# Loading each 128-token chunk of q, k and v head by head, one contiguous 32 KB block per transfer

## The chip, the cores and the metric

The kernel runs on one core of one Trainium2 chip. The metric is the device time of one execution in microseconds (us). A run has a profile as well; its **span** is the time from the first to the last instruction of the program and is 1.6 to 2.2 us shorter than the run's time in all runs below. Fast executions of one kernel differ by up to 2%, and each job ran the kernel before again on its own chip (133.4 to 136.5 us), so changed kernels are compared with the runs of before of the same job.

## The reference, cut to what matters

The first half is a retention recurrence over q, k, v of shape (4 batches, 8 heads, 768 tokens, 64), the second a token mixer on its output.

```python
for t in range(S):
    state = gamma[None, :, None, None] * state + np.einsum('bhd,bhe->bhde', k[:, :, t], v[:, :, t])
    y[:, :, t] = scale * np.einsum('bhd,bhde->bhe', q[:, :, t], state)
# ... y is rearranged to x[b, s, h*d]
W_tok = scale * np.einsum('bsd,btd->bst', x @ w_q, x @ w_k)   # 1 / sqrt(64), as above
return (np.maximum(np.einsum('bst,btd->bsd', W_tok, x), 0.0) @ w_out)
```

## The kernel before

The recurrence is worked in chunks of 128 tokens: 4 batches x 6 chunks = 24 chunks. A chunk of q, k or v becomes a tile of 128 partitions (tokens) by 8 heads x 64 floats. In HBM the head is the outer dimension, so within one head the 128 tokens of a chunk are contiguous (128 x 64 x 4 bytes = 32 KB), and the eight heads are eight such blocks. One load takes all eight:

```python
    def emit_dma(i):                       # chunk i
        b, c = divmod(i, NCH)
        q_st = stage_pool.tile([128, H, D], FP32, name="q_st", tag="stage")   # 15 buffers: 5 chunks
        # ... k_st, v_st likewise
        nc.sync.dma_start(
            out=q_st,
            in_=q[b, :, c * C : (c + 1) * C, :].rearrange("h t d -> t h d"),
        )
        # ... k and v likewise, 256 KB each
```

GpSimd scales and casts q and k to bf16 and ScalarE casts v; TensorE transposes, scores and accumulates; VectorE and ScalarE empty its results. The stores of the mixer go through the same queue (SyncE's, called SP in the profile) as the loads:

```python
            nc.sync.dma_start(out=out[b, tc_i * C : (tc_i + 1) * C, :], in_=o_st)   # [128, 512] f32, 256 KB
    # ...
    for i in range(NG):
        # ... emit_dma(i + 3), emit_cast(i + 2), emit_tr(i + 1), emit_scores(i), emit_y(i - 1), ...
        # ... and, in iterations 1 to 4 of a batch, the mixer and the stores of the batch before
```

The queue carries its instructions out in order: in the trace before, a store stands from 54.83 us, the two after it wait for their results and start at 58.31 and 58.76, and the next load starts behind them, at 59.23. Eight completion semaphores are used in turn (in the trace before, 99 DMAs on 101 to 106, 108 and 110), so that a DMA waits until the DMA eight before it has landed: each of the 91 from the ninth on waits for the semaphore of the DMA eight before it, and none was issued before that had landed.

Of the kernel before, what the change touches and what calls it, by code (L numbers as in the profile page):

```python
# [17 lines left out]
def kernel(  # L18
# [10 lines left out]
    nc = tc.nc  # L29

    B, H, S, D = q.shape
    DM = moe_w_out.shape[0]
    DH = moe_w_q.shape[1]
    C = 128
# [37 lines left out]
    for c in range(NCH):  # L72
        nc.vector.tensor_scalar_mul(
            out=txln[:, c, :], in0=ln_gamma, scalar1=tvals_f[:, c : c + 1]
# [9 lines left out]
        out=cmask,  # L84
        in_=cmask,
# [9 lines left out]
    for i in range(NUM_U):  # L95
# [15 lines left out]
        out=wout_stage, in_=moe_w_out.rearrange("(a p) m -> p a m", p=128)  # L111
# [16 lines left out]
    def emit_dma(i):  # L128
        b, c = divmod(i, NCH)
        st = cctx[i]  # L130
        q_st = stage_pool.tile([128, H, D], FP32, name="q_st", tag="stage")
        k_st = stage_pool.tile([128, H, D], FP32, name="k_st", tag="stage")
        v_st = stage_pool.tile([128, H, D], FP32, name="v_st", tag="stage")
        nc.sync.dma_start(  # L134
            out=q_st,
            in_=q[b, :, c * C : (c + 1) * C, :].rearrange("h t d -> t h d"),
        )
        nc.sync.dma_start(  # L138
            out=k_st,
            in_=k[b, :, c * C : (c + 1) * C, :].rearrange("h t d -> t h d"),  # L140
        )
        nc.sync.dma_start(  # L142
            out=v_st,
            in_=v[b, :, c * C : (c + 1) * C, :].rearrange("h t d -> t h d"),
        )
        st["q_st"] = q_st
        st["k_st"] = k_st
        st["v_st"] = v_st
# [250 lines left out]

    alloc_batch(0)  # L400
    emit_dma(0)
    emit_dma(1)
    emit_cast(0)
    emit_dma(2)
    emit_cast(1)
    emit_tr(0)

    for i in range(NG):
        b, c = divmod(i, NCH)
# [60 lines left out]
```

## Time and profile before

| | before |
|---|---|
| time, median of 2 runs | 136.5 us (135.25 to 137.76) |
| span of the profiled run | 132.4 us |
| TensorE (PE) busy | 97.8 us, 74% of the span |
| load instructions on SyncE's queue | 72, of 256 KB |
| median from issue to landing | 4.2 to 4.3 us |
| packets on the load queue | 79,920 |
| share of the 16 DMA engines' time | 79.6% |

From the list of what SyncE's queue itself waited for (us in total, times, longest): the stores stand between the loads and wait for their results.

```profile
SPq L391 <- DVE o_st L388: 32.1, 8, 11.3
```

Of these 32 us the most lie after the last load, where nothing is behind them; the others delay loads.

### The profile page before, as it was taken

The page shows a single profiled execution, that of the slowest core. Times are in us where ns is not written, and L with a number is a line of the kernel's source. Part 1 is how long each engine was busy: PE and PEld are TensorE (multiplying, and loading weights), DVE is VectorE, ACT ScalarE, POOL GpSimd, SP SyncE. Part 2 cuts the span into 40 slices and gives each one's busy share as a digit, 9 for nine tenths or more (in the row PEclk, how much of TensorE's full clock was granted, in tenths as well). Part 3 has the DMA queues.
Part 4 walks back from the last instruction along what each step waited for, and adds up shares of the span by engine and source line. Part 5 has one row for each costly group of instructions (what it writes and reads, how often), then busy time and mean ns, then how long its engine had stood idle before and what let it go on. Part 6 is the DMA issues. An engine that isn't in the chain of part 4 may idle for free.

```text
span 132.4 us, 2906 instructions
## 1 busy us (share of the span) xinstructions
PE 97.8 (74%) x1128; PEld 64.1 (48%) x1128; DVE 78.6 (59%) x141; ACT 58.3 (44%) x127; POOL 50.9 (38%) x65
## 2 busy tenths in 40 slices
PE   0003679765699899981799899861999999977970
PEld 0002558544478466560476556541675556653320
DVE  4061654975767599393457797590637797551830
ACT  3002454653556645382315757362325657413430
POOL 4009755467627654240765550425754200000000
PEclk9999999999999999999779999998569999999999
DMA  3899999999979998959999839959998006600074
GB/s 83 289 272 247 240 245 228 225 246 246 270 168 229 240 226 261 237 168 272 254 244 251 196 83 303 251 172 268 260 223 197 0 4 235 241 0 0 5 296 179
DMA packets 79933, 26.66 MB, mean 201 GB/s; under 512 B 76336, under 2 KB 76336, under 8 KB 79920
## 3 DMA queue, kind: packets, MB, share of 16 engines
q1 hardware_dynamic: 79920, 26.48, 79.6%
q8 instruction: 9, 0.15, 0.4%
q14 instruction: 4, 0.03, 0.1%
HBM read 20.19 MB, written 6.29 MB: 200 GB/s over the span
## 4 chain that ended last, share of the span: by engine, by line
PE 52%; SPq 16%; DMA 13%; ACT 4%; DVE 4%; POOL 4%; issue 3%; POOLq 0%; ACTq 0%; DVEq 0%
PE o_ps L379 13%; DMA q_st<-in_q_dram 12%; SPq L142 6%; PE wqt_ps L308 6%; PE z_ps L342 5%; PE mx_ps L358 4%; PE at_ps L211 4%; SPq L134 4%; PE tr_ps L181 3%; PE xt_ps L285 3%; PE y_ps L269 3%; SPq L138 3%; POOL qs L156 3%; PE wk_ps L322 3%; PE y_ps L261 3%
## 5 line engine op out<-in xcount | busy, mean ns | idle before, releaser
L221 DVE TENSOR_TENSOR at_sb<-at_ps,cmask 128x512 bf16<-128x512 f32 x48 | 31.0, 684 | 25.0 <-PE at_ps L211 25.0
L156 POOL TENSOR_TENSOR qs<-q_st,fq 128x512 bf16<-128x512 f32 x24 | 25.0, 1042 | 48.2 <-DMA q_st<-in_q_dram 33.3
L276 ACT CAST x_nat<-y_ps 128x512 bf16<-128x512 f32 x24 | 14.0, 585 | 29.5 <-PE y_ps L269 29.4
L162 POOL TENSOR_TENSOR ks<-k_st,fk 128x512 bf16<-128x512 f32 x24 | 25.0, 1042 | 3.6 <-DMA k_st<-in_k_dram 2.5
L181 PE MATMUL tr_ps<-identity,qs 128*128 128x128 bf16 x96 | 10.5, 239 | 20.4 <-POOL qs L156 20.3
L379 PE MATMUL o_ps<-wout_sb,relu_mx 128*128 128x512 bf16 x96 | 22.4, 379 | 0.0
L199 DVE COPY qkt<-tr_ps 128x1024 bf16<-128x1024 bf16 x24 | 16.4, 681 | 4.3 <-PE tr_ps L190 4.3
L181 PEld LDWEIGHTS <-qs 128*128 128x128 bf16 x96 | 6.9, 106 | 23.7 <-POOL qs L156 21.6
L168 ACT ACTIVATE vs<-v_st 128x512 bf16<-128x512 f32 x24 | 15.2, 632 | 0.3 <-DMA v_st<-in_v_dram 0.3
L367 DVE TENSOR_SCALAR relu_mx<-mx_ps 128x512 bf16<-128x512 f32 x16 | 9.9, 683 | 8.0 <-PE mx_ps L358 8.0
L379 PEld LDWEIGHTS <-relu_mx 128*128 128x128 bf16 x96 | 8.9, 98 | 9.8 <-DVE relu_mx L367 1.1
L238 PE MATMUL state_ps<-vs,ks 128*128 128x128 bf16 x80 | 8.6, 232 | 4.8 <-ACT vs L168 2.8
L190 PE MATMUL tr_ps<-identity,ks 128*128 128x128 bf16 x96 | 10.7, 242 | 1.1 <-POOL ks L162 1.1
L269 PE MATMUL y_ps<-vs,at_sb 128*128 128x64 bf16 x192 | 11.1, 201 | 0.0
L247 ACT CAST u_tile<-state_ps 64x256 bf16<-64x256 f32 x20 | 7.3, 365 | 8.3 <-PE state_ps L238 8.3
L211 PE MATMUL at_ps<-qkt 64*128 64x128 bf16 x192 | 10.6, 233 | 0.4 <-DVE qkt L199 0.4
L285 PE MATMUL xt_ps<-identity,x_nat 128*128 128x128 bf16 x96 | 10.0, 228 | 1.2 <-ACT x_nat L276 1.1
L388 DVE COPY o_st<-o_ps 128x512 f32<-128x512 f32 x12 | 8.2, 686 | 3.8 <-PE o_ps L379 2.1
L390 ACT COPY o_st<-o_ps 128x512 f32<-128x512 f32 x12 | 7.0, 584 | 7.3 <-PE o_ps L379 5.7
L308 PE MATMUL wqt_ps<-x_t,wq_sb 128*64 128x256 bf16 x48 | 9.2, 342 | 0.3 <-DVE x_t L296 0.3
L238 PEld LDWEIGHTS <-ks 128*128 128x128 bf16 x80 | 5.9, 105 | 7.1 <-issue 7.0
L261 PE MATMUL y_ps<-u_tile,qkt 128*128 128x128 bf16 x80 | 9.3, 226 | 0.0
(37 smaller groups left out, 101.1 us busy)
## 6 DMA issues: line engine op xcount, KB each, us to landing
q_st<-in_q_dram SPq DMA_DIRECT2D x24, 256.0 KB, 4.3
k_st<-in_k_dram SPq DMA_DIRECT2D x24, 256.0 KB, 4.2
v_st<-in_v_dram SPq DMA_DIRECT2D x24, 256.0 KB, 4.3
out_dram<-o_st SPq DMA_DIRECT2D x24, 256.0 KB, 2.3
wout_stage<-in_moe_w_out_dram SPq DMA_DIRECT2D x1, 1024.0 KB, 5.9
wq_stage<-in_moe_w_q_dram SPq DMA_DIRECT2D x1, 128.0 KB, 2.2
wk_stage<-in_moe_w_k_dram SPq DMA_DIRECT2D x1, 128.0 KB, 2.4
```

Source lines behind the costliest of these rows:

```text
L156: nc.gpsimd.tensor_tensor(out=qs, in0=st["q_st"], in1=fq[:, c, :].to_broadcast([128, H, D]), op=ALU.mult,)
L162: nc.gpsimd.tensor_tensor(out=ks, in0=st["k_st"], in1=fk[:, c, :].to_broadcast([128, H, D]), op=ALU.mult,)
L168: nc.scalar.activation(out=vs, in_=st["v_st"], func=ACT.Copy, scale=float(attn_scale))
L181: nc.tensor.matmul(out=tr_ps[:, hp, :], lhsT=qs[:, 2 * hp : 2 * hp + 2, :], rhs=identity, is_transpose=True, start=True, stop=True,)
L199: nc.vector.tensor_copy(out=qkt, in_=tr_ps)
L211: nc.tensor.matmul(out=ps[:, j, :], lhsT=kT(qkt, h), rhs=qT(qkt, h), start=(j == 0), stop=(j == 3),)
L221: nc.vector.tensor_tensor(out=at_sb_par[:, parity, :, :], in0=at_ps[parity], in1=cmask.to_broadcast([128, 4, C]), op=ALU.mult,)
L238: nc.tensor.matmul(out=state_ps[:, hp, :, :], lhsT=ks[:, 2 * hp : 2 * hp + 2, :], rhs=vs[:, 2 * hp : 2 * hp + 2, :], start=(c == 0 and hp ...
L269: nc.tensor.matmul(out=y_ps[:, h, :], lhsT=at_sb[:, h, :], rhs=vs[:, h, :], start=(c == 0 and h == 0), stop=(h == H - 1),)
L276: nc.scalar.copy(out=x_nats[b][:, c, :], in_=y_ps)
L308: nc.tensor.matmul(out=wqt_ps, lhsT=wq_sb[:, dmc, :], rhs=x_t[:, dmc, blk * 2 * C : (blk + 1) * 2 * C], start=(dmc == 0), stop=(dmc == NDM ...
L379: nc.tensor.matmul(out=o_ps, lhsT=relu_mx[:, dmc, tc_i * C : (tc_i + 1) * C], rhs=wout_sb[:, dmc, :], start=(dmc == 0), stop=(dmc == NDM - 1),
```

## The change

The intent: each transfer reads one unbroken 32 KB block of HBM in place of eight blocks. Nothing else changes.

```diff
-        nc.sync.dma_start(
-            out=q_st,
-            in_=q[b, :, c * C : (c + 1) * C, :].rearrange("h t d -> t h d"),
-        )
+        for h in range(H):
+            nc.sync.dma_start(
+                out=q_st[:, h, :], in_=q[b, h, c * C : (c + 1) * C, :]
+            )
 # ... the same for k and v
```

More of the change, by code (lines that the diff above doesn't have):

```diff
@@ L133, in emit_dma @@
         v_st = stage_pool.tile([128, H, D], FP32, name="v_st", tag="stage")
-        nc.sync.dma_start(
-            out=q_st,
-            in_=q[b, :, c * C : (c + 1) * C, :].rearrange("h t d -> t h d"),
-        )
-        nc.sync.dma_start(
-            out=k_st,
-            in_=k[b, :, c * C : (c + 1) * C, :].rearrange("h t d -> t h d"),
-        )
-        nc.sync.dma_start(
-            out=v_st,
-            in_=v[b, :, c * C : (c + 1) * C, :].rearrange("h t d -> t h d"),
-        )
+        for h in range(H):
+            nc.sync.dma_start(
+                out=q_st[:, h, :], in_=q[b, h, c * C : (c + 1) * C, :]
+            )
+        for h in range(H):
+            nc.sync.dma_start(
+                out=k_st[:, h, :], in_=k[b, h, c * C : (c + 1) * C, :]
+            )
+        for h in range(H):
+            nc.sync.dma_start(
+                out=v_st[:, h, :], in_=v[b, h, c * C : (c + 1) * C, :]
+            )
         st["q_st"] = q_st
```

## The prediction

> **What bounds the kernel now.** I read the page from the engines to the transfers, then the chain of work that ended last, then the issues and the SyncE queue's own timeline. First the page: busy time by engine, the slices in time, the packets, the chain.
>
> ```profile
> PE 97.8 (74%) x1128; PEld 64.1 (48%) x1128; DVE 78.6 (59%) x141; ACT 58.3 (44%) x127; POOL 50.9 (38%) x65
> ...
> DMA  3899999999979998959999839959998006600074
> GB/s 83 289 272 247 240 245 228 225 246 246 270 168 229 240 226 261 237 168 272 254 244 251 196 83 303 251 172 268 260 223 197 0 4 235 241 0 0 5 296 179
> DMA packets 79933, 26.66 MB, mean 201 GB/s; under 512 B 76336, under 2 KB 76336, under 8 KB 79920
> ...
> q1 hardware_dynamic: 79920, 26.48, 79.6%
> ...
> PE 52%; SPq 16%; DMA 13%; ACT 4%; DVE 4%; POOL 4%; issue 3%; POOLq 0%; ACTq 0%; DVEq 0%
> ```
>
> No engine is full (PE 74%). The DMA row reads 8 or 9 for most of the first 31 of 40 slices (3.31 us each, so to about 103 us), at roughly 250 GB/s: while loads run, the transfers set the pace, and the last 29 us are PE work on what was loaded. The packet count can be taken apart exactly. 72 loads x 8 heads x 128 tokens is 73,728 packets of 256 B; the two small weights make 1,024 more; 99 DMAs with 16 completion packets each make 1,584. The sum is 76,336, the "under 512 B" figure to the unit. So today's load is already cut into 256 B pieces, one token of one head. In the chain, SPq and DMA together have 29% of 132.4 us, 38 us: no better way of loading can save more along this chain.
>
> The list of issues, with KB each and median us to landing:
>
> ```profile
> q_st<-in_q_dram SPq DMA_DIRECT2D x24, 256.0 KB, 4.3
> k_st<-in_k_dram SPq DMA_DIRECT2D x24, 256.0 KB, 4.2
> v_st<-in_v_dram SPq DMA_DIRECT2D x24, 256.0 KB, 4.3
> out_dram<-o_st SPq DMA_DIRECT2D x24, 256.0 KB, 2.3
> wout_stage<-in_moe_w_out_dram SPq DMA_DIRECT2D x1, 1024.0 KB, 5.9
> wq_stage<-in_moe_w_q_dram SPq DMA_DIRECT2D x1, 128.0 KB, 2.2
> ```
>
> And what one issue holds the SyncE queue for (timeline of that queue; start, us held, what, count):
>
> ```profile
> 22.63 1.62 SPq L142 DMA_DIRECT2D v_st<-in_v_dram  x1
> 24.34 0.86 SPq L134 DMA_DIRECT2D q_st<-in_q_dram  x1
> ...
> 50.67 0.38 SPq L391 DMA_DIRECT2D out_dram<-o_st  x1
> ...
> 58.31 0.36 SPq L391 DMA_DIRECT2D out_dram<-o_st  x1
> 59.23 0.41 SPq L134 DMA_DIRECT2D q_st<-in_q_dram  x1
> ...
> 125.71 0.33 SPq L391 DMA_DIRECT2D out_dram<-o_st  x1
> ```
>
> These rows carry the prediction. With transfers backed up (22 to 25 us) a 1,024-piece load holds the queue 0.8 to 1.6 us[...]. Directly after a pause (59.23) the same 1,024-piece load takes 0.41 us, and a 128-row store 0.33 to 0.38. An eighth of the pieces saves under 0.1 us: an issue costs about 0.35 us **per instruction**, nearly whatever it moves.
>
> [...]
>
> **The change part by part.**
>
> Removed: 72 load issues of 256 KB. Added: 72 x 8 = 576 issues of 32 KB. All stay on the SyncE queue; the instruction listing shows 601 rows on it instead of 101.
>
> Pieces: the HBM side becomes contiguous, but the tile still takes 64 floats, 256 B, into each of 128 partitions, so I expect the same 73,728 packets of 256 B, plus (603 - 99) x 16 = 8,064 completion packets: 87,984 on the load queue. One load gives each DMA engine 8 + 1 packets. Between 20 and 50 us the queue moved 232 GB/s with the engines full, 256 B x 16 / 232 GB/s = 17.7 ns per packet; 9 of them are 0.16 us. The transfer is then shorter than its issue, and the DMA engines sit idle over half of the time.
>
> Pitch of issues: a load behind another starts 0.04 to 0.05 us after it ends (first rows of that timeline: 2.38 + 0.51 to 2.93, 7.70 + 0.85 to 8.60). The closest likeness to the new load is the 128-row store: 0.38 back to back, 0.36 or 0.33 after a pause. I choose 0.38 + 0.05 = **0.43 us**. Two stores in a row stood 0.45 us apart (50.22, 50.67), with one wait more each.
>
> Load stream: 576 x 0.43 = 247.7 us. Ahead of the last load lie 12 stores of the first two batches, 12 x 0.45 = 5.4 us. First load issued at 2.4 us. Last load issued at about 255.5, landed 2 us later (2.2 us for today's 128 KB weight on a free queue): 257.5 us. I add nothing for stores that block the queue (32 us today waiting for o_st): a chunk now comes every 24 x 0.43 = 10.3 us, while PE's work for one is 97.8 / 24 = 4.1 us, and in the listing what those stores need hangs on a chunk loaded at least 10 us earlier.
>
> Tail: only the last chunk's remaining work follows. Before, its scores began at 113.2 and the span ended at 132.4: 19.2 us of scores, transposes, the last batch's mixer, stores. v lands last and goes through one 0.63 us cast. PE has been half idle, and after idle waits its transposes took 0.40 us per four instead of 0.22 (63.78 against 69.22 in the chain), so I add 1 us for a slow start. 257.5 + 0.6 + 19.2 + 1 = 278.3 us of span.
>
> Before, the timed median exceeds the span by 136.5 - 132.4 = 4.1 us. Sum: **282 us**, about 2.07 times the time before. None of the added issue time is hidden: the queue needs 248 us for loads alone, more than the whole kernel today. What it gives back, the load wait of 38 us in the chain, is already gone from this sum, because PE's earlier work lies inside the load stream.
>
> **The rivals.**
>
> A. The contiguous reads pay: pieces merge into larger ones and the DMA-bound first 100 us shrink. For it: 250 GB/s is well under the 303 GB/s of one slice. Against: SBUF's side stays at 256 B, and the issue cost stands anyway. Taken alone, without issue cost, it would give at best 136.5 - 38 = 98 us.
>
> B. Issue time is per piece, not per instruction. For it: the usual 0.85 us for 1,024 pieces, 0.11 us for 128; then 576 x 0.11 = 63 us hide beside transfers and the time stays within 2%, 134 to 139 us. Against: 0.41 us for 1,024 pieces on a free queue and 0.33 for 128 rows.
>
> C. Latency takes over from issue. In the listing each DMA waits until the DMA eight before it has landed, so at most 8 x 32 KB are in flight where it was 8 x 256 KB. If a landing still took 4.3 us, the pitch would be 4.3 / 8 = 0.54 us, and 576 of them 310 us: about 344 us in all. Against: landing on a free queue is 2.0 to 2.4 us, a pitch of 0.25 to 0.30, below the issue's own.
>
> D. The pitch is nearer the first issues of the program (0.43 to 0.58 us): at 0.52 us it is 300 us of loads and about 334 in all. For the low end, 0.33 + 0.04 = 0.37 us, loads take 213 us and the whole 247.
>
> **Range and chances.** Everything but the pitch sums to about 34 us. The pitch from 0.38 to 0.50 us gives 253 to 322; I set 252 to 322 for 8 in 10, the middle at 282. Faster by 2% would need both the issue rows and the packet count misread: 0.01. Within 2% needs rival B: 0.02. Slower: 0.97.
>
> **What would show it right or wrong.** Right: 576 load issues of 0.33 to 0.42 us standing back to back from 2.4 to about 255 us; DMA row at 3 to 5 throughout, about 75 GB/s; landing near 2 us; about 87,984 packets on the load queue; the chain mostly SPq at the load lines, with PE only in the last 20 us; PE busy under 45%. Rival C shows as landings over 3.4 us and the queue waiting on DMA; rival A as fewer packets or over 300 GB/s in a window; rival B as issues of about 0.1 us. The point fails if the small load's issue differs from the store's, or if stores block the queue for many us.

The 282 us are 2.4 + 247.7 + 5.4 to the last issue (255.5), 2 for its landing, 0.6 + 19.2 + 1 of tail and 4.1 from span to time, and the pitch of 0.43 us is the 0.38 + 0.05 read from the trace. The completion packets are the packets of 4 B on the load queue: 1,584 before and 9,648 after, 16 per DMA, and after there are as many semaphore updates by DMAs (9,648). The 8 + 1 packets per DMA engine are an estimate, the 144 packets of a load divided by the 16 engines of the page; the trace does not tell a packet's engine.

## The result, and the profile after

The changed kernel takes **317.32 us** (316.88 and 317.77), against 136.5 us: slower by a factor of 2.33 (2.28 to 2.39). Ratios here are the mean time of one kernel's fast runs over that of the other's of the same rounds, so they are not quite the ratio of the medians quoted. Executions over 1.5% slower than the fastest of the same kernel are left out of the means. Kernels are compared only within the same rounds.

The page of the profile after: engines, slices in time, packets, load queue, and the shares of the chain that ended last.

```profile
PE 135.2 (43%) x1128; PEld 83.4 (26%) x1128; DVE 82.4 (26%) x141; ACT 61.5 (20%) x127; POOL 51.5 (16%) x65
...
DMA  6333332333322332333244332333253522332515
GB/s 196 67 70 69 69 70 62 69 69 69 69 64 60 70 68 62 70 69 69 60 153 132 92 71 62 69 68 71 63 155 68 154 65 65 70 69 63 182 51 202
DMA packets 88003, 26.74 MB, mean 85 GB/s; under 512 B 84400, under 2 KB 84400, under 8 KB 87984
...
q1 hardware_dynamic: 87984, 26.52, 33.7%
...
SPq 79%; issue 9%; DMA 4%; PE 4%; DVE 1%; ACT 1%; POOLq 0%; POOL 0%; ACTq 0%
```

Where the DMA row read 8 or 9 it now reads 2 or 3: the DMA engines have nothing to do for two thirds of the time, and no compute engine is over 43% busy. The chain is the SyncE queue, 79% of the span, which was 16%. PE's busy time rose by 37 us with the same 1,128 matmuls, because each takes longer (300 ns in the mean, 248 before); the row of the granted clock reads 5 to 7 tenths over much of the second half (0.62 to 0.67 in the stretches from 150 to 290 us). PE is not in the way, with 4% of the chain, so this costs little.

The list of issues of the profile after (count, KB each, median us to landing), and one line's own view (duration of one in ns, least, median, longest):

```profile
q_st<-in_q_dram SPq DMA_DIRECT2D x192, 32.0 KB, 1.9
```

```profile
L135 SPq DMA_DIRECT2D q_st<-in_q_dram x192: 327/430/1587, 2.4 to 285.1; - x192
```

And the chain in order of time, at the start of the last q and k loads (start, us, what):

```profile
281.33 0.43 SPq L143
281.76 0.05 issue
281.81 0.02 SPq L135
281.83 0.03 issue
281.86 0.38 SPq L135
282.23 0.04 issue
282.28 0.43 SPq L135
282.71 0.04 issue
282.75 0.43 SPq L135
...
288.92 3.17 DMA k_st<-in_k_dram
```

This is the whole loss in small: 0.43 us of issue and 0.04 us before the next, 0.47 us from start to start, and nothing else between. It goes on from 2.4 us to the last load at 294.1 us. A landing takes 1.9 us from issue, while the load that waits for it comes eight places, 8 x 0.474 = 3.8 us, later: the limit of eight in flight does not bind.

The trace holds every packet. The median 256 B packet took 18 ns before and 18 ns after (means 18.0 and 17.4 ns; 74,752 packets in each). **The contiguous blocks made no packet faster.** The load before reads the same eight 32 KB blocks, and both cut them into 256 B, one head's floats of one token. In these two traces a data packet of the load queue is as long as the run that is unbroken both in HBM and within one partition of the tile: 256 B for the loads, and 2 KB for the 24 stores and the weight w_out (3,584 packets), although each store writes one unbroken 256 KB block of HBM.

Where the 182.5 us between the two spans come from: before, 98.4 us until the last load is issued and 34.0 after it; after, 294.1 us and 20.9. The load stream grew by 196 us, and the tail gave back 13, since less work is still waiting when the last chunk arrives.

### The profile page after: what moved, and what is told of

It is laid out like the page before. It is cut to its first block, busy times and chain, and to the rows that moved or that the text cites. A ratio compares the mean times of both kernels' runs of the same rounds, so it can differ in the third digit from the quotient of the medians.

```text
span 314.9 us, 3693 instructions
## 1 busy us (share of the span) xinstructions
PE 135.2 (43%) x1128; PEld 83.4 (26%) x1128; DVE 82.4 (26%) x141; ACT 61.5 (20%) x127; POOL 51.5 (16%) x65
## 2 busy tenths in 40 slices
DMA packets 88003, 26.74 MB, mean 85 GB/s; under 512 B 84400, under 2 KB 84400, under 8 KB 87984
## 3 DMA queue, kind: packets, MB, share of 16 engines
q1 hardware_dynamic: 87984, 26.52, 33.7%
## 4 chain that ended last, share of the span: by engine, by line
SPq 79%; issue 9%; DMA 4%; PE 4%; DVE 1%; ACT 1%; POOLq 0%; POOL 0%; ACTq 0%
SPq L135 26%; SPq L139 26%; SPq L143 25%; DMA wout_stage<-in_moe_w_out_dram 2%; SPq L391 2%; PE o_ps L379 1%; DMA k_st<-in_k_dram 1%; DMA out_dram<-o_st 1%; DMA v_st<-in_v_dram 0%; PE z_ps L342 0%; PE mx_ps L358 0%; DVE at_sb L221 0%; POOLq L465 0%; PE wqt_ps L308 0%; POOL ks L162 0%
## 5 line engine op out<-in xcount | busy, mean ns | idle before, releaser
L181 PE MATMUL tr_ps<-identity,qs 128*128 128x128 bf16 x96 | 14.2, 300 | 119.8 <-POOL qs L156 119.8
L379 PE MATMUL o_ps<-wout_sb,relu_mx 128*128 128x512 bf16 x96 | 29.5, 451 | 0.0
L238 PE MATMUL state_ps<-vs,ks 128*128 128x128 bf16 x80 | 11.1, 274 | 31.4 <-ACT vs L168 31.4
L190 PE MATMUL tr_ps<-identity,ks 128*128 128x128 bf16 x96 | 13.5, 289 | 19.8 <-POOL ks L162 19.5
L238 PEld LDWEIGHTS <-ks 128*128 128x128 bf16 x80 | 8.1, 124 | 35.1 <-issue 34.8
L190 PEld LDWEIGHTS <-ks 128*128 128x128 bf16 x96 | 8.3, 127 | 27.7 <-POOL ks L162 26.9
L269 PE MATMUL y_ps<-vs,at_sb 128*128 128x64 bf16 x192 | 14.8, 240 | 0.4 <-DVE at_sb L221 0.4
L211 PE MATMUL at_ps<-qkt 64*128 64x128 bf16 x192 | 14.6, 301 | 0.0
L285 PE MATMUL xt_ps<-identity,x_nat 128*128 128x128 bf16 x96 | 14.2, 301 | 0.5 <-ACT x_nat L276 0.5
L269 PEld LDWEIGHTS <-at_sb 128*128 128x128 bf16 x192 | 12.9, 133 | 1.4 <-issue 0.8
L388 DVE COPY o_st<-o_ps 128x512 f32<-128x512 f32 x12 | 8.2, 691 | 13.4 <-PE o_ps L379 7.6
L296 DVE COPY x_t<-xt_ps 128x1024 bf16<-128x1024 bf16 x12 | 8.3, 692 | 12.9 <-PE xt_ps L285 12.9
```

What stands on the lines that cost most here:

```text
L181: nc.tensor.matmul(out=tr_ps[:, hp, :], lhsT=qs[:, 2 * hp : 2 * hp + 2, :], rhs=identity, is_transpose=True, start=True, stop=True,)
L190: nc.tensor.matmul(out=tr_ps[:, HP + hp, :], lhsT=ks[:, 2 * hp : 2 * hp + 2, :], rhs=identity, is_transpose=True, start=True, stop=True,)
L238: nc.tensor.matmul(out=state_ps[:, hp, :, :], lhsT=ks[:, 2 * hp : 2 * hp + 2, :], rhs=vs[:, 2 * hp : 2 * hp + 2, :], start=(c == 0 and hp ...
L269: nc.tensor.matmul(out=y_ps[:, h, :], lhsT=at_sb[:, h, :], rhs=vs[:, h, :], start=(c == 0 and h == 0), stop=(h == H - 1),)
L379: nc.tensor.matmul(out=o_ps, lhsT=relu_mx[:, dmc, tc_i * C : (tc_i + 1) * C], rhs=wout_sb[:, dmc, :], start=(dmc == 0), stop=(dmc == NDM - 1),
```

## The experiments

The theory: an issue costs its queue some 0.47 us whatever it moves, and 576 of them in one queue are the time. The rivals: the cost goes with the pieces; contiguous or small reads are themselves slow or fast; the limit of eight in flight; something that all queues share. Twelve kernels were run; all gave correct results.

### Fewer, larger issues: two heads per load

```diff
-        for h in range(H):
-            nc.sync.dma_start(out=q_st[:, h, :], in_=q[b, h, c * C : (c + 1) * C, :])
+        for h in range(0, H, 2):
+            nc.sync.dma_start(out=q_st[:, h : h + 2, :],
+                in_=q[b, h : h + 2, c * C : (c + 1) * C, :].rearrange("h t d -> t h d"))
```

> Two heads per load: 288 loads of 64 KB (256 pieces of 256 B each) in place of 576 of 32 KB. Theory 'cost per issue on the SyncE queue' (0.474 us start to start, nearly whatever a load moves): 288 x 0.474 = 136.5 us of loads, + 12 stores 5.6, + about 6 us of scattered stalls, + 2.4 start, + 2 landing, + 19 tail: span about 172 us, time 170 to 182, issues still about 0.43 us long. Rival 'cost per 256 B piece in the issue': the number of pieces is unchanged, so the issues double in length to about 0.86 us and the time stays near 317. Rival 'eight loads in flight': no change of pitch at all as long as a landing (1.9 us) is under eight pitches; if it were the limit, pitch stays and time halves likewise, so this run does not test that one.

Measured: 191.8 us (191.3 and 192.3), 1.44 times before (1.427 to 1.457). The issue line's view:

```profile
L135 SPq DMA_DIRECT2D q_st<-in_q_dram x96: 396/468/1591, 2.4 to 162.9; - x96
```

Twice the pieces lengthen an issue from 430 to 468 ns, not to 860: the cost is per instruction, and the rival of cost per piece falls. The time lies 10 us above the expected range and the span, 190.5 us, 18.5 above the expected 172. Of these, 11 are the pitch (start to start), which was 0.512 us and not 0.474: 288 x 0.038 = 11 us; the others are about 5.5 us of stalls beyond the 6 allowed for, and a tail 2 us longer. So an issue isn't quite independent of what it moves.

### Four heads per load

The same edit with steps of 4.

> Four heads per load: 144 loads of 128 KB. Theory: 144 x 0.474 = 68 us of issue, below the about 83 us that the DMA engines need for the 73,728 pieces (18 ns each over 16 engines), so the transfers bound it again and the time is that of the kernel before within 2 to 3%: 134 to 141 us. Rival 'splitting as such costs' (completion packets, waits, smaller loads): between the two, above 145 us. Rival 'contiguity pays, when issue does not hide it' : it would show as under 133 us, though this load is only half way there (32 KB blocks, four per load).

Measured: fast runs 135.5 and 137.5 us, ratio 1.026 (1.012 to 1.041); median of all four runs 137.9 us, two of them slow. The pitch is 0.55 us; 144 x 0.55 = 79 us of issue, about what the DMA engines need (an estimate of 83 us, 73,728 packets of 18 ns over 16 engines), so the queue and the transfers are level, and the profile (a slow run) reads 217 and 221 GB/s in the stretches from 20 to 50 and from 60 to 80 us. The large loss is gone. Some 2 to 3% remain, which speaks for "splitting as such costs" in a small size, and there is no sign of a gain from contiguity.

### v from another queue

```diff
-            nc.sync.dma_start(out=v_st[:, h, :], in_=v[b, h, c * C : (c + 1) * C, :])
+            nc.scalar.dma_start(out=v_st[:, h, :], in_=v[b, h, c * C : (c + 1) * C, :])
```

> The changed kernel with the 192 v loads issued from ScalarE's queue and 384 q and k loads left on SyncE's. Theory 'cost belongs to the issuing queue': SyncE needs 384 x 0.474 = 182 us + 5.6 for stores + about 8 stalls + 2.4 + 2 + 19, span about 219, time 212 to 230; ScalarE has 58 us of work plus 192 x 0.45 = 86, 144 in all, not the bound. Rival 'a descriptor generator or the DMA engines shared by both queues sets the pitch of 0.474': the sum over both queues keeps it, time stays near 310 to 317. A caveat: both queues draw on the same eight completion semaphores, and ScalarE's loads stand in order behind its own work, so a result between the two is possible; then the pitch within SyncE's undisturbed stretches decides.

Measured: 240.6 us (238.3 and 242.9; the second, profiled, counts as slow). That is above the expected 212 to 230 but far below 310. Timelines of both queues of this kernel, a stretch in which both issue (start, us from the first start to the last end, what, count):

```profile
31.81 1.85 SPq L139 DMA_DIRECT2D k_st<-in_k_dram  x4
```

```profile
31.90 0.83 ACTq L143 DMA_DIRECT2D v_st<-in_v_dram  x2
32.78 0.93 ACTq L143 DMA_DIRECT2D v_st<-in_v_dram  x2
```

SyncE's four loads stand (1.85 - 0.43) / 3 = 0.47 us apart while ScalarE issues four of its own. In the whole trace 92 pitches of SyncE's loads lie where ScalarE was issuing for over 80% of the time: their median is 0.474 us, as without. So the cost belongs to the issuing queue; a limit at this rate that both queues share is ruled out. What was lost against 219 us of expected span is what the caveat named: waits for landings, which the changed kernel does not have.

```profile
SPq L135 <- DMA v_st<-in_v_dram: 9.1, 6, 2.6
SPq L139 <- DMA k_st<-in_k_dram: 7.3, 25, 0.6
SPq L135 <- DMA k_st<-in_k_dram: 2.7, 8, 0.4
```

With eight semaphores for two queues each queue has about four, an estimate, and 4 x 0.474 = 1.9 us is just a landing (1.9 us in the changed kernel). These three rows are 19 us, and 219 + 19 is within 3 us of the measured span, 240.9.

### The same number of issues, without the contiguous block

```diff
-        for h in range(H):
-            nc.sync.dma_start(out=q_st[:, h, :], in_=q[b, h, c * C : (c + 1) * C, :])
+        for s in range(8):
+            nc.sync.dma_start(out=q_st[16 * s : 16 * s + 16, :, :],
+                in_=q[b, :, c * C + 16 * s : c * C + 16 * s + 16, :].rearrange("h t d -> t h d"))
```

> The same number of loads (576 of 32 KB, 128 pieces of 256 B), but each takes 16 tokens of all eight heads, so it reads eight separate 4 KB blocks in place of one of 32 KB, and fills 16 partitions in place of 128. Theory 'only the number of issues counts': the time of the changed kernel within 2%, 311 to 324 us, 18 ns per piece. Rival 'contiguous 32 KB reads are worth something (or cost something) themselves': more than 2% away from 317 us and pieces that take longer than 18 ns.

Measured: 317.5 us (315.8 to 318.5 in 4 fast runs), the changed kernel's time to within 0.1%; 2.386 times before. The issue line's view:

```profile
L135 SPq DMA_DIRECT2D q_st<-in_q_dram x192: 311/429/1617, 2.4 to 285.3; - x192
```

The pitch is 0.473 us and the median packet 18 ns. Eight separate 4 KB blocks per transfer or one of 32 KB: no difference. This and the run with two heads settle it: the contiguous read is neutral, and the number of instructions is what was paid for.

### Stores on ScalarE's queue, loads as before

```diff
-            nc.sync.dma_start(out=out[b, tc_i * C : (tc_i + 1) * C, :], in_=o_st)
+            nc.scalar.dma_start(out=out[b, tc_i * C : (tc_i + 1) * C, :], in_=o_st)
```

> The kernel before, with the 24 stores issued from ScalarE's queue, so that no load waits behind a store that waits for its result (SyncE waited 32 us for o_st before, in 8 waits). Theory 'the load queue is what the first 100 us wait for': loads run on at the transfer rate (73,728 pieces x 18 ns / 16 = 83 us plus 6 us of stores plus weights), the last load is issued near 90 us in place of 98, and the time falls by 4 to 8 us, to 126 to 130 us. Rival 'PE or the fixed order of PE bounds those stretches anyway': within 2% of before, 131 to 136 us.

Measured: 132.2 us (131.7 to 132.6, 4 fast runs) against 134.0, ratio 0.987 (0.979 to 0.994). It is faster than both kernels, by 1.3% (0.6 to 2.1) than the one before, which is less than expected. The reason given for it failed: the last load is issued at 100.5 us, not near 90. Loads now wait for the landing of stores instead, as the list of SyncE's waits shows:

```profile
SPq L134 <- DMA out_dram<-o_st: 13.7, 2, 7.2
```

So a store on the other queue still holds up loads on this one: 13.7 us in two waits, as it holds one of the eight semaphores from which the loads draw.

### Stores on GpSimd's queue

The same edit with `nc.gpsimd`.

> The same with the stores issued from GpSimd's queue in place of ScalarE's. Theory as for that run, 126 to 132 us; GpSimd has 51 us of work, but its casts stand in order behind stores that wait for o_st, which can delay the next chunk's cast. If that is the limit, 133 us or more.

Measured: median 135.1 us (131.9 to 137.4), three of the four runs slow. The profile (a slow run) is of use all the same: the last load is issued at 89.1 and lands at 93.9 us, 9 us earlier than before (98.4 and 103.0), yet the last chunk's scores start at 111.9 us (before 113.2). This run does not show what earlier loads are worth, because the stores now stand before GpSimd's casts and wait there:

```profile
POOL out_dram L391 <- ACT o_st L390: 29.7, 7, 11.0
```

The last chunk's k was cast at 107.9 us, behind such a store, and at 102.4 before. What is known of the end comes from the kernel before: there that cast was done at 103.5 us, 9.7 before the scores, and TensorE was busy for 12.6 of the 13 us from 100 to 113. So the arrival of the last chunk did not set the end.

### Only v head by head

```diff
+        nc.sync.dma_start(out=q_st, in_=q[b, :, c * C : (c + 1) * C, :].rearrange("h t d -> t h d"))
+        # ... k_st likewise
         for h in range(H):
             nc.sync.dma_start(out=v_st[:, h, :], in_=v[b, h, c * C : (c + 1) * C, :])
```

> Only v is loaded head by head; q and k stay whole: 192 loads of 32 KB and 48 of 256 KB, 240 issues. The corrected model (0.474 us start to start for a 32 KB load, 0.55 to 0.6 for a 256 KB load on a free queue, 12 stores of 0.45, about 6 us of stalls at instruction fetches): 192 x 0.474 = 91 + 48 x 0.58 = 28 + 5.6 + 6 + 2.4 = 133 us to the last load, + 2 + 19 = 154 of span, time 150 to 162. Rival 'the cost is proportional to the share of transfers that are contiguous or small' (a third of the loss of the full change): 134 + 184 / 3 = 195 us. Rival 'transfers hide it': under 140 us.

Measured: median 175.3 us (three fast runs of 174.5 to 175.9, a slow one of 177.8), 1.31 times before. No rival was right and the model neither: it is 13 us above the top of its range, though still 20 us below the rival of a third of the loss. The last load is issued at 148.5 us in place of 133. The timeline of its queue, individual issues of one chunk read from the trace (start, us held):

```
68.28 0.38 q, 256 KB    68.76 0.53 k, 256 KB    69.38 0.98 first v, 32 KB    70.41 0.42 second v
```

After two 256 KB loads the first small one is held for about a microsecond (median of 24: 0.97; what holds it is not shown), which adds some 0.5 us per chunk, 24 times, or 12 us. Here the sum of issues alone was too small; where sizes alternate, something came on top. The "instruction fetches" of this expectation and the next are the 16 KB packets of the queue that the page calls instruction; in the changed kernel eight issues of 1.2 to 2.1 us lie beside one each (9.3 us in all, see below), and the 6 and 16 us are estimates.

### Smaller loads still: 64 tokens of one head

```diff
         for h in range(H):
-            nc.sync.dma_start(out=q_st[:, h, :], in_=q[b, h, c * C : (c + 1) * C, :])
+            for t0 in (0, 64):
+                nc.sync.dma_start(out=q_st[t0 : t0 + 64, h, :],
+                    in_=q[b, h, c * C + t0 : c * C + t0 + 64, :])
```

> Each 32 KB load cut in two again: 1,152 loads of 16 KB (64 tokens of one head, 64 pieces). The pitch so far: 0.55 us at 512 pieces, 0.512 at 256, 0.474 at 128, that is 0.038 less for each halving. Theory 'almost all of an issue is fixed': 0.436 us at 64 pieces, 1,152 x 0.436 = 502 us, + 12 stores 5.6, + about 16 of stalls at instruction fetches, + 2.4 + 2 + 19: span about 547, time 530 to 565. Rival 'an issue costs in proportion to its pieces below 128': the pitch halves to 0.24 us and the time stays at 317.

Measured: 777.9 us (777.7 and 778.1). The rival is far off, but so is the expected 547: the issue of half as many bytes takes longer.

```profile
L136 SPq DMA_DIRECT2D q_st<-in_q_dram x384: 465/595/705, 2.4 to 731.3; - x192
```

The pitch is 0.639 us, and 1,152 x 0.639 = 736 us. A landing takes 2.1 us here, under 8 x 0.639, so again no wait for landings. Two runs followed to find what made it dear.

### 64 tokens of two heads, and 32 tokens of four

```diff
+        for h in range(0, H, 2):               # and, in the second kernel, steps of 4
+            for t0 in range(0, C, 64):         # and steps of 32
+                nc.sync.dma_start(out=q_st[t0 : t0 + 64, h : h + 2, :], ...)
```

> 576 loads of 32 KB and 128 pieces again, but each 64 tokens (64 partitions) of two heads. The 16 KB load of 64 tokens of one head stood 0.639 us apart, more than the 32 KB load of 128 tokens (0.474) and of 16 tokens of eight heads (0.473). Reading 1, 'a 64-partition destination is dear': pitch near 0.64 to 0.68, time near 415. Reading 2, 'what counts is how many pieces each DMA engine gets, and fewer than eight is dear': here again eight pieces per engine, pitch 0.474, time 315 to 320.

> The same count and size with 32 tokens of four heads. Reading 2 (pieces per engine): pitch 0.474, time 315 to 320. Reading 1 in a wider form ('partition counts between 16 and 128 are dear'): pitch of 0.5 us or more, time above 330.

Measured, one look each: 417.1 and 317.2 us. The issue lines' views, of the first and of the second kernel:

```profile
L136 SPq DMA_DIRECT2D q_st<-in_q_dram x192: 595/605/1319, 2.4 to 383.2; - x192
```

```profile
L136 SPq DMA_DIRECT2D q_st<-in_q_dram x192: 311/430/1572, 2.4 to 285.2; - x192
```

Both loads are 32 KB in 128 pieces, eight per engine if they are spread evenly over the 16. With 32 partitions (as with 16 and with 128) the issue takes 430 ns, with 64 it takes 605, and from start to start 0.47 and 0.65 us. So it goes with the shape of 64 tokens (64 partitions of the tile, and 64 rows of the source), and not with the number of pieces per engine. Which side of the transfer counts and why 64 is dear stay open.

### An earlier start

Weights loaded after the third chunk and cast in the fourth iteration, with the stores on ScalarE's queue (first) and on SyncE's (second).

```diff
-    nc.sync.dma_start(out=wq_stage, ...)       # three weights, then their three casts,
-    nc.vector.tensor_copy(out=wq_sb, ...)      # ahead of everything
     emit_dma(0)
     emit_dma(1)
     emit_cast(0)
     emit_dma(2)
+    nc.sync.dma_start(out=wq_stage, ...)       # three loads here, three casts when i == 3
```

> A version meant to beat both: whole 256 KB loads as before, stores from ScalarE's queue, and the mixer's weights loaded after the third chunk and cast in the fourth iteration, so that VectorE's txln (at 8.9 us before, behind the 1.2 us cast of the weight that landed at 7.7) and with it the first cast of q no longer wait for 1 MB of weights. Theory: the first q cast starts near 6 us in place of 10.1, so 3 to 5 us less than with the stores moved alone: 127 to 130 us. Rival 'the start is hidden again later by what bounds the middle': as with the stores moved alone, 131 to 133 us.

> The same late weights with the stores left on SyncE's queue. Theory: 129 to 132 us against 134 before, the early start alone giving 3 to 5 us. Rival: the loads' blocking behind stores takes the gain back, 133 to 135 us.

Measured: 134.2 us (132.3 to 136.3) against 135.9, fast runs 0.984 times before (0.971 to 0.996); and 137.5 us (135.7 to 138.2), 1.011 times (1.001 to 1.022). The first cast of q did move, from 10.1 to 3.9 us, further than expected, and the last chunk's scores start at 112.9 (a slow run) and 116.0 us (113.2 before). Six microseconds won at the start were lost on the way. In both the rival was nearer, by the ratio; the times themselves lie above the rivals' ranges too, in a job whose kernel before took 135.9 us and not 134. The first of the two equals, within its interval, the kernel with the stores moved alone, which is the simplest one that is faster than both kernels. What bounds the middle of the kernel before was not followed further.

## Why the prediction was right, point by point

The forecast was slower, near 282 us in a range of 252 to 322; 317.3 us came, inside the range but close to its top. The mechanism was right, and a term of the sum was too small. The range was made of the pitch alone (0.38 to 0.50 us); that the stalls found below, which were not in it, still fitted under its top was luck.

- **Issues per instruction, one queue solid from 2.4 us to the end of the loads**: right. The chain has SPq at 79%, the line of issues 430 ns with 32 KB, 468 with 64 KB. Landing near 2 us: 1.9. PE under 45%: 43%. Load queue: 87,984 packets, as computed, to the unit. The DMA row at 3 to 5 was read a little high (2 to 3, 67 to 70 GB/s).
- **The term that failed: "I choose 0.38 + 0.05 = 0.43 us"** for the pitch. It is 0.474, which makes 576 x 0.044 = 25 us. The 0.38 us came from stores, and a store has two waits. The first is a separate instruction on the queue (24 for 24 stores, 17 ns each), and the chain after shows what that does: a load that has one (281.81, 0.02 us) takes 0.38, the load after it, with its one wait inside, 0.43, and with the gaps both come to the same. The prediction took the shorter duration of the one form and the shorter gap of the other. The trace before had the right number, in rows that were passed over; here three stores in a row and the load that follows them (timeline of SyncE's queue, before):

```profile
78.64 0.36 SPq L391 DMA_DIRECT2D out_dram<-o_st  x1
79.09 0.38 SPq L391 DMA_DIRECT2D out_dram<-o_st  x1
79.59 0.39 SPq L391 DMA_DIRECT2D out_dram<-o_st  x1
80.08 0.41 SPq L134 DMA_DIRECT2D q_st<-in_q_dram  x1
```

  From start to start 0.45, 0.50 and 0.49. The prediction quoted one such distance, 0.45, the first after a pause, which is the shortest. And the load at 59.23, which it calls "directly after a pause", stands 0.47 us behind a store at 58.76 that its excerpt leaves out.
- **A term that was missing: scattered stalls.** The stream of loads and 12 stores took 292.1 us; 588 x 0.474 is 278.7. Of the other 13.4 us, 1.4 is one wait for the landing of a weight and 2.7 are twelve small delays; 9.3 are what eight issues of 1.2 to 2.1 us took beyond 0.474 from start to start, and each of them lies beside one 16 KB packet of the instruction queue (8 of 8, at 47.1, 92.9, 124.0, 152.8, 191.8, 219.4, 258.1 and 289.6 us by the packet records). The page's line for that queue, after:

```profile
q8 instruction: 9, 0.15, 0.2%
```

  The packets take 0.95 to 1.52 us, and each of the eight issues ends 0.37 to 0.39 us after its packet does (0.35 to 0.41 in the run with 1,152 loads, again 8 of 8), so the issue waits until the packet is through; by what path isn't shown. The packets come 228 to 274 TensorE instructions (matmuls and weight loads) apart, and there are nine of them with 99 DMAs on SyncE's queue as with 603, so they are probably TensorE's instructions and not SyncE's own.
- **The tail**: 0.6 + 19.2 + 1 predicted from the last landing; 314.9 - 296.0 = 19.0 measured. The extra 1 us for a cold PE was not needed.
- **Span to time**: 4.1 us taken from a median and a span of different executions. A run's own difference is 2 us (316.9 - 314.9).
- **Stores do not block the queue**: right. SyncE waited 11.1 us for o_st, 8.7 of it in one wait after the last load.
- **Rival A (contiguity)**: refuted by 18 ns per packet before and after and by the token split's equal time. Its ceiling of 38 us, read from the chain, was not tested. It is a share of the chain, and what removing it would give can be less: in the kernel before, the last chunk's k was cast 9.7 us before its scores began.
- **The listing**: the prediction reads 601 rows on SyncE's queue against 101; the traces have 603 DMAs against 99, which are the counts that its packet sum uses.
- **Rival B (per piece)**: refuted by two heads per load. **Rival C (landing)**: 1.9 us against 3.8; it did appear when two queues shared the semaphores. **Rival D (a pitch of 0.52)**: nearest to the truth in size, though the issues at the start of the program were not its reason.

The sum redone: 2.4 + 292.1 to the end of the last issue, 1.5 to its landing, 19.0 of tail, 2.0 between this run's span and its time: 317.0 us, where that run took 316.9.

## What to carry to other kernels

Before splitting a transfer, count the instructions it puts on one queue and multiply them by the distance from start to start of that queue's issues, read in the middle of a run of issues and not after a pause; here 576 x 0.474 us outweighed everything the transfers did. A contiguous block in HBM bought nothing here, where the run that goes into one SBUF partition stayed the same (longer runs were not tried); look at the packet sizes and their duration before and after. If transfers have to be small, the loss all but ends where issue time falls under transfer time (here at 128 KB, 1.026 times before; at 64 KB it was still 1.44 times), and a second queue helps only as far as its completion semaphores allow (here from 317 to 241 us, with 19 us of waits for landings).
